# Attention with two MoE-style layers on one core: g_q and g_k issued by ScalarE, the function table loaded by a small first Square, the first pair's roots on VectorE, the second pair's q and k loaded ahead of v

## The chip, the cores and the metric

The program runs on one core of one Trainium2 chip. The metric is device time in microseconds (us) of one execution. The time before is 1150.96 us, the median of three runs (1147.56 to 1157.47).

## What is computed

Attention with normalized q and k, and then two feed-forward layers over its output.

```python
# q, k, v: (4, 12, 448, 64) float32; g_q, g_k: (64,)
def rmsnorm(x, g):
    return x / np.sqrt(np.mean(x * x, axis=-1, keepdims=True) + 1e-06) * g
scores = (q_n @ k_n.T) / sqrt(64)          # q_n = rmsnorm(q, g_q), k_n = rmsnorm(k, g_k)
attn = softmax(scores);  x = attn @ v      # per batch and head
x = x.transpose(0, 2, 1, 3).reshape(1792, 768)
h = x @ moe_w_in;   g = h * sigmoid(1.702 * h);                      x = g @ moe_w_out
h = x @ moe2_w_in;  g = max(h, 0) + moe2_alpha * min(h, 0);          out = g @ moe2_w_out
```

The four weight matrices (768 x 2048 into a layer, 2048 x 768 out of it) come in as 64-bit floats, all other inputs as 32-bit floats.

## The kernel before

**Tiles and stages.** Heads are handled in pairs: a batch of 12 heads has 6 pairs, and one pair's q and k make one tile `qk` of 128 partitions x 2 heads x 7 column groups x 64. The first batch's attention is computed in 32-bit floats, the later batches' in halves of 16 bits. The weights are read as 32-bit words (`weights`, from line 203; a load is issued at line 223), converted by ScalarE and VectorE into 32-bit floats (`from_words`: lines 148, 164, 165), measured by row (line 245), and split into a high and a low 16-bit part (lines 179, 180). The loop over the first batch's first half units is woven with the conversion of the first weight matrix, three steps of it for each attention step; the maximum of v for the later batches is measured in between (lines 312, 314). Then the first feed-forward layer, the other batches' attention beside it, and the second layer follow.

**The first microseconds.** The program makes the identity and the ones, loads the first pair's q and k (`load_qk`, four DMAs, lines 378 to 381), then calls `gains`, which loads g_q and g_k to all partitions (lines 282, 283), multiplies them (284), takes the largest product (287), makes a power of two of it and its reciprocal (105, 106, 112, 113), scales the product (293), and has TensorE transpose it into a column `g_col` (296, 297). v of the first pair comes next (`load_v`, lines 394 to 397), then the second pair's q and k, its v, and the weights. `normalize(0)` squares the first pair's q and k on ScalarE (line 421, two halves), adds them up on VectorE (423), and takes inverse roots on GpSimd by three Newton steps, 14 small operations (424 to 434). `prep_pair(0)` multiplies q and k by the roots (`qn`, line 458), transposes them on TensorE (465, 467), evacuates them on ScalarE with `g_col` as the scale (468), and takes the maximum of v on VectorE (470). The scores (516) follow.

**What sets the order.** All loads at the head go through SyncE's queue, which issues in order; a DMA whose buffer is not free, or that must wait for another, holds all those behind it. On each engine the instructions run in the order in which they were issued, and that order is not the written one: the program is traced in its written order, and a planner (`schedule_with_timeline_sim=True`) places the instructions of each engine by a timeline of its own, the earlier written first among those that are ready there. `issue_after` ties an instruction behind another; the loads that measure v wait so for the roots of pair 4. ScalarE's function table is loaded by an instruction that the build puts ahead of the first activation.

Of the kernel before, what the change touches and what calls it, by code (L numbers as in the profile page):

```python
# [9 lines left out]
F32 = mybir.dt.float32  # L10
# [47 lines left out]
def attention_moe_kernel(  # L58
# [220 lines left out]
    def gains():  # L279
        gq = small.tile([128, D], F32, tag="gq", name="gq", bufs=1)  # L280
        gk = small.tile([128, D], F32, tag="gk", name="gk", bufs=1)
        nc.sync.dma_start(out=gq, in_=g_q.partition_broadcast(128))
        nc.sync.dma_start(out=gk, in_=g_k.partition_broadcast(128))
        nc.vector.tensor_tensor(out=gq, in0=gq, in1=gk, op=ALU.mult)
        gm = small.tile([128, 1], F32, tag="gm", name="gm", bufs=1)
        gi = small.tile([128, 1], F32, tag="gi", name="gi", bufs=1)
        nc.vector.tensor_reduce(out=gm, in_=gq, op=ALU.max, axis=AX, apply_absolute_value=True)
        pow2floor(c_s, gm)
        scaled_reciprocal(gi, c_s, 0.5)
        nc.vector.memset(gs[64:128, 3], 1.0)  # L290
        for c in range(4):
            ps = slice(0, 64 if c == 3 else 128)
            nc.vector.tensor_scalar(out=gs[ps, c], in0=gq[ps], scalar1=gi[ps], scalar2=None, op0=ALU.mult)
        nc.vector.tensor_scalar(out=c_s, in0=c_s, scalar1=2.0 ** -22, scalar2=None, op0=ALU.mult)
        gt = ps_m.tile([128, 128], F32, tag="m", name="gt")
        nc.tensor.transpose(out=gt, in_=gs[:, 0:2].rearrange("p c d -> p (c d)"), identity=identf)
        nc.scalar.activation(out=g_col, in_=gt[:, 0:1], func=AF.Copy, scale=c_s)
# [111 lines left out]
    def normalize(*Ps):  # L409

        Ps = [P for P in Ps if P < B * NP]
        if not Ps:
            return
        n = NT2
        w = 2 * n * len(Ps)
        ss = small.tile([128, 4 * NT2], F32, tag="ss", name="ss")[:, 0:w]
        for t, P in enumerate(Ps):
            flat = raws[P].rearrange("p h c d -> p (h c) d")
            for i in range(2):
                sq = att_p.tile([128, n, D], F32, tag="sq", name="sq", bufs=SQB)  # L420
                nc.scalar.activation(out=sq, in_=flat[:, i * n:(i + 1) * n], func=AF.Square, scale=2.0 ** -13)
                o = (2 * t + i) * n
                nc.vector.tensor_reduce(out=ss[:, o:o + n], in_=sq, op=ALU.add, axis=AX)
        nc.gpsimd.tensor_scalar(out=ss, in0=ss, scalar1=1e-6 * 2.0 ** -20, scalar2=None, op0=ALU.add)
        rs = small.tile([128, 4 * NT2], F32, tag="rs", name="rs")[:, 0:w]
        tn = small.tile([128, 4 * NT2], F32, tag="tn", name="tn")[:, 0:w]
        nc.gpsimd.tensor_scalar(
            out=rs.bitcast(I32), in0=ss.bitcast(I32), scalar1=-0.5, scalar2=RSQRT_SEED, op0=ALU.mult, op1=ALU.add
        )
        for _ in range(3):  # L430
            nc.gpsimd.tensor_tensor(out=tn, in0=rs, in1=rs, op=ALU.mult)
            nc.gpsimd.tensor_tensor(out=tn, in0=tn, in1=ss, op=ALU.mult)
            nc.gpsimd.tensor_scalar(out=tn, in0=tn, scalar1=-0.5, scalar2=1.5, op0=ALU.mult, op1=ALU.add)
            rooted[Ps[0]] = nc.gpsimd.tensor_tensor(out=rs, in0=tn, in1=rs, op=ALU.mult)
        for t, P in enumerate(Ps):
            eng = side(P)
            ks = raws[P][:, :, 0:4]
            flat = raws[P].rearrange("p h c d -> p (h c) d")
            root = rs[:, 2 * n * t:2 * n * (t + 1)]
            if P < NP:  # L440
                roots[P] = root
                continue
            eng.tensor_tensor(out=ks, in0=ks, in1=gs.unsqueeze(1).to_broadcast([128, 2, 4, D]), op=ALU.mult)
            eng.tensor_tensor(out=flat, in0=flat, in1=root.unsqueeze(2).to_broadcast([128, 2 * n, D]), op=ALU.mult)
# [737 lines left out]
    if True:  # L1182
        make_identity(nc, ident)
        nc.vector.memset(ones, 1.0)
        nc.vector.tensor_copy(out=identf, in_=ident)
        load_qk(0)
        gains()
        load_v(0)
        load_qk(1)
        load_v(1)  # L1190
        g0 = big.tile([128, KF, 2, S], F16, tag="g", name="g0")
        stage = g0.rearrange("p m e t -> p (m e t)").bitcast(F32)
        parts = stage[:, 0:R1I * 1024].bitcast(I32).rearrange("p (i n t) -> p i n t", i=R1I, t=2)
        raw1o = g0.rearrange("p m e t -> p m (e t)").bitcast(I32)[:, KF - 4 * R1O:, FIRST:].rearrange("p m (n t) -> p m n t", t=2)

        def num1i(j):
            if j == KD - 1:
                return stage[:, 5120:5120 + FF]
            return held.bitcast(F32)[:, (j - 3) * FF:(j - 2) * FF]

        def num1o(j):
            if j == KF - 2:
                return att_p.tile([128, 2 * NT2 * D], F32, tag="ph", name="num1o", bufs=PHB)[:, 0:DM]
            return raw_p.tile([128, 2 * NT2 * D], F32, tag="qk", name="num1o", bufs=QKB)[:, 0:DM]

        w1i_steps = weights(
            moe_w_in, "w1i", lambda: w1i, later_rows(w1i, 3, num1i), lambda t: parts[:, t % R1I], 4, R1I, 2.0 ** -14, scales,
            G1I
        )
        w1o_steps = weights(  # L1210
            moe_w_out, "w1o", lambda: w1o, later_rows(w1o, 2, num1o), lambda t: raw1o[:, 4 * (t % R1O):4 * (t % R1O) + 4], 2,
            R1O, 2.0 ** -25, scales, G1O
        )
        next(w1i_steps)
        normalize(0)
        for _ in prep_pair(0):
            pass
        for P in range(2, 1 + QKB):
            load_qk(P)
        load_v(2)  # L1220
        normalize(1)
        early = measure(1, B - 1, 4)
        for i, _ in enumerate(first_pairs()):
            if i >= 6:
                for _ in range(1):
                    next(early, None)
            for _ in range(W_RATE):
                next(w1i_steps, None)
        for _ in w1i_steps:
            pass  # L1230
        v_scales(0, v0)
        first_x()
        moe1_scales(0)
        for P in range(NP, NP + 2):
            load_qk(P)
            load_v(P)
        n1o = 0
        steps = attention([4 * P + r for P in range(NP) for r in range(2, 4)])
        for i, _ in enumerate(steps):
            pairs = max(0, (i - LAG + 1) // 2)  # L1240
            rows = KF - 2 if pairs >= 4 else (HOLD + pairs * HELD) // (2 * DM) - 2
            while n1o < min(1 + 2 * rows + 3 * (rows // 2), (i + 1) * W1O_RATE, 57):
                next(w1o_steps)
                n1o += 1
            if i >= M_AT and i - M_AT < KF:
                first_in(slice(0, FIRST), i - M_AT, g0)
            for _ in range(2):
                next(early, None)
        while n1o < 57:
            next(w1o_steps)  # L1250
            n1o += 1
        for m in range(len(range(2 * NP + LAG)) - M_AT, KF):
            first_in(slice(0, FIRST), m, g0)
        with tc.issue_after(loads["w1o"][W1O_HOLD].ins):
            normalize(NP, NP + 1)
            for _ in prep_pair(NP):
                pass
            load_qk(NP + 2)
            load_qk(NP + 3)
            load_v(NP + 2)  # L1260
        att_steps = other_batches()
        done = 4 * NP
        late = late_weights(ctx, att)
        for b in range(B):
            last = min(NU, 4 * NP * (b + 2)) + LAG2
            first = done
            got = None
            for i, _ in enumerate(moe1(b) if b else first_moe1(g0)):
                lead = 0 if b else B1_AT
                want = first + (last - first) * min(1.0, max(0.0, i + 1 - lead) / (PACE[b] * TICKS - lead))  # L1270
                while done < min(want, NU + LAG2):
                    next(att_steps)
                    done += 1
                if b == B - 1:
                    for _ in range(1 if i < 2 * KF else 2):
                        if got is None or i >= 2 * KF:
                            got = next(late, None)
        second_layer(late)
# [30 lines left out]
```

## Time and profile before

| what | value |
|---|---|
| median of three runs | 1150.96 us |
| profiled execution, its own time | 1150.36 us |
| span of its profile | 1148.6 us |
| TensorE matmul busy | 1069.4 us, 93% |
| VectorE busy | 802.1 us, 70% |
| ScalarE busy | 693.2 us, 60% |
| GpSimd busy | 179.4 us, 16% |

The span is the time between the first and the last instruction that the profile shows; the profiled execution's own time is 1.8 us longer. PE is TensorE's matmul, PEld its weight load, DVE is VectorE, ACT is ScalarE, POOL is GpSimd, SP is SyncE and SPq its queue of DMA issues. A busy share over the whole span mixes stages of different limits, so the stretches are read one by one.

### The profile page before, as it was taken

How to read it: one execution, taken by the hardware profiler on the slowest of the kernel's cores; microseconds unless marked ns; L12 is line 12 of the kernel's file. 1: busy time of each engine (PE TensorE's matmuls, PEld its weight loads, DVE VectorE, ACT ScalarE, POOL GpSimd, SP SyncE). 2: the span in 40 equal slices, each digit the busy share in tenths (PEclk: the TensorE clock that was granted, in tenths of full speed). 3: DMA queues.
4: the chain of work that ended last, by engine and by line, in shares of the span. 5: the costliest groups of instructions: out<-in, count | busy, mean ns of one | idle time of the engine just before them, and what ended most of it. 6: DMA issues, size and time to landing. Idle time of an engine off the chain costs nothing.

```text
span 1148.6 us, 18408 instructions
## 1 busy us (share of the span) xinstructions
PE 1069.4 (93%) x6753; PEld 585.0 (51%) x6753; DVE 802.1 (70%) x1397; ACT 693.2 (60%) x1452; POOL 179.4 (16%) x364
## 2 busy tenths in 40 slices
PE   4776889898989999999999999999999999999998
PEld 2343457744444445555455455444444477666664
DVE  5979798887879885577534865599976224959341
ACT  4778686888879876688633562356456425756120
POOL 2701003676433342100000000000000000000000
PEclk9978899899999999999999999999999999999999
DMA  7974743478888756455446501765351423363111
GB/s 227 258 178 132 182 129 109 97 158 184 183 191 167 160 130 151 109 121 118 78 124 229 203 1 64 249 215 194 136 171 59 138 70 113 106 184 101 33 31 28
DMA packets 235562, 158.19 MB, mean 138 GB/s; under 512 B 167888, under 2 KB 214736, under 8 KB 235472
## 3 DMA queue, kind: packets, MB, share of 16 engines
q1 hardware_dynamic: 229200, 141.34, 44.6%
q0 software_dynamic: 6272, 15.67, 5.3%
q8 instruction: 53, 0.87, 0.3%
q14 instruction: 37, 0.30, 0.1%
HBM read 92.35 MB, written 25.69 MB: 103 GB/s over the span
## 4 chain that ended last, share of the span: by engine, by line
PE 56%; DVE 16%; DMA 11%; issue 7%; ACT 6%; POOL 4%; SPq 1%; DVEq 0%; POOLq 0%; ACTq 0%
PE op L1090 17%; PE yp L821 15%; PE h L927 9%; PE hp L798 7%; PE xp L648 3%; PE sp L525 2%; DMA t<-hl 2%; PE hp L758 2%; DMA g<-in_moe_w_in_dram 2%; DVE nm L530 1%; DMA g<-in_moe_w_out_dram 1%; DVE g L141 1%; ACT pr L550 1%; DMA qk<-in_q_dram 1%; DMA yr<-y_dram 1%
## 5 line engine op out<-in xcount | busy, mean ns | idle before, releaser
L821 PE MATMUL yp<-g,w1o 128*128 128x448 f16 x1152 | 226.9, 354 | 1.5 <-DVE g L767 0.9
L927 PE MATMUL h<-x,w2i 128*128 128x512 f16 (+1 forms) x1152 | 219.3, 352 | 4.3 <-DVE pos L933 2.8
L798 PE MATMUL hp<-x,w1i 128*128 128x448 f16 x864 | 170.3, 353 | 1.6 <-DVE t L807 1.6
L927 PEld LDWEIGHTS <-w2i 128*128 128x128 f16 x1152 | 112.6, 98 | 109.6 <-issue 5.1
L821 PEld LDWEIGHTS <-w1o 128*128 128x128 f16 x1152 | 109.5, 98 | 110.8 <-issue 12.0
L798 PEld LDWEIGHTS <-w1i 128*128 128x128 f16 x864 | 81.9, 98 | 83.5 <-issue 9.6
L620 DVE SCALAR_TENSOR_TENSOR ph<-pr,sm,ph 128x448 f16<-128x448 f32 x126 | 85.2, 707 | 25.4 <-ACT ph L593 25.4
L530 DVE TENSOR_REDUCE nm<-sp 128x2 f32<-128x896 f32 x96 | 92.5, 964 | 10.3 <-PE sp L525 7.6
L932 ACT ACTIVATE pos<-h,sign 128x512 f32<-128x512 f32 (+1 forms) x64 | 40.1, 628 | 89.7 <-PE h L927 83.3
L550 ACT ACTIVATE pr<-sp,nm,c_s 128x448 f32<-128x448 f32 x126 | 89.9, 717 | 2.4 <-DVE ph L620 1.1
L1090 PEld LDWEIGHTS <-even 128*128 128x128 f16 x672 | 65.7, 98 | 43.5
L933 DVE SCALAR_TENSOR_TENSOR pos<-h,slope,pos 128x512 f32<-128x512 f32 (+1 forms) x64 | 43.4, 680 | 59.9 <-ACT pos L932 59.7
L593 ACT ACTIVATE ph<-pr,sm 128x448 f16<-128x448 f32 x126 | 77.6, 659 | 10.7 <-DVE sm L590 10.6
L758 PE MATMUL hp<-x,w1i 128*128 128x256 f16 (+1 forms) x576 | 66.1, 276 | 9.2 <-DVE g L767 5.2
L1090 PEld LDWEIGHTS <-odd 128*128 128x128 f16 x504 | 49.3, 98 | 32.6
L758 PEld LDWEIGHTS <-w1i 128*128 128x128 f16 x576 | 55.2, 104 | 20.2 <-issue 14.8
L1090 PE MATMUL op<-w2lo,even 128*128 128x384 f16 x384 | 63.5, 326 | 0.0
L648 PE MATMUL xp<-pt,vs 128*64 128x256 f16 (+1 forms) x792 | 49.8, 267 | 7.5 <-DMA pt<-ph 6.2
L525 PE MATMUL sp<-t 64*128 64x448 f16 (+1 forms) x432 | 54.0, 357 | 0.6 <-DMA t<-hl 0.5
L648 PEld LDWEIGHTS <-vs 128*64 128x64 f16 x792 | 37.9, 112 | 27.6 <-issue 17.2
L532 ACT ACTIVATE nm<-nm,c_s 128x2 f32<-128x2 f32 x72 | 20.9, 290 | 48.5 <-DVE nm L530 48.1
L1090 PE MATMUL op<-w2hi,even 128*128 128x384 f16 x288 | 47.5, 326 | 0.0
(243 smaller groups left out, 1659.7 us busy)
## 6 DMA issues: line engine op xcount, KB each, us to landing
g<-in_moe_w_in_dram SPq DMA_DIRECT2D x24, 512.0 KB, 6.1
g<-in_moe_w_out_dram SPq DMA_DIRECT2D x32, 384.0 KB, 4.0
w2raw<-in_moe_w_in_dram SPq DMA_DIRECT2D x24, 512.0 KB, 5.7
w2raw<-in_moe_w_out_dram SPq DMA_DIRECT2D x16, 768.0 KB, 6.4
g_dram<-pos SPq DMA_DIRECT2D x48, 256.0 KB, 2.0
gp<-g_dram SPq DMA_DIRECT2D x8, 1024.0 KB, 6.8
odd<-g_dram SPq DMA_DIRECT2D x6, 1024.0 KB, 5.5
y_dram<-y SPq DMA_DIRECT2D x24, 224.0 KB, 2.5
```

Source lines behind the costliest of these rows:

```text
L525: nc.tensor.matmul(out=sp[:, j, 0:S] if n == 2 else sp[ds, 0, 0:S], lhsT=qt[ds] if n == 2 else qt[ds, 64:128], rhs=kt[ds, 0:S], start=(i = ...
L530: nc.vector.tensor_reduce(out=nm[:, 0:n], in_=sp[:, 0:n, 0:S], op=ALU.max, axis=AX, negate=True)
L550: last = nc.scalar.activation(out=pr[i], in_=sp[:, i, 0:S], func=AF.Exp, bias=nm[:, i:i + 1], scale=c_s if u >= 4 * NP else 1.0, accum_out ...
L593: nc.scalar.activation(out=ph[:, i, 0:S], in_=pr[i], func=AF.Copy, scale=sm[:, i:i + 1])
L620: nc.vector.scalar_tensor_tensor(out=ph[:, i, S:2 * S], in0=pr[i], scalar=sm[:, i:i + 1], in1=ph[:, i, 0:S], op0=ALU.mult, op1=ALU.subtract)
L648: nc.tensor.matmul(out=xp[64 * j:64 * j + 64, t:t + n], lhsT=vs[ks, j, c], rhs=pt[ks, 7 * j + kc, 0:n] if b else pt[ks, kc, o:o + n], star ...
L758: nc.tensor.matmul(out=ps, lhsT=w1i[:, kk, e, m * 128:(m + 1) * 128], rhs=xs[0, kk][:, f, cols], start=(i == 0), stop=(i == 3 * KD - 1))
L798: nc.tensor.matmul(out=ps, lhsT=w1i[:, kk, e, m * 128:(m + 1) * 128], rhs=x[:, f], start=(n == 0), stop=(n == 3 * KD - 1))
L821: nc.tensor.matmul(out=ps, lhsT=w1o[:, m, e, j * 128:(j + 1) * 128], rhs=g[:, m, f], start=(n == 0), stop=(n == 3 * KF - 1))
L927: nc.tensor.matmul(out=ps, lhsT=w2i[:, kk, e, m * 128:(m + 1) * 128], rhs=x2[kk][:, f], start=(c == 0), stop=(c == 3 * KD - 1))
L933: nc.vector.scalar_tensor_tensor(out=pos, in0=ps, scalar=slope[:, m:m + 1], in1=pos, op0=ALU.mult, op1=ALU.max)
L1090: nc.tensor.matmul(out=ps, lhsT=ops[:, o, m, f], rhs=rhs[:, e], start=(c == 0), stop=(c == 3 * KH - 1))
```

## The change

Four edits. `gains` issues the loads of g_q and g_k from ScalarE's queue, no longer from SyncE's, and is called after `normalize(0)` instead of after `load_qk(0)`. The first pair's roots are computed by VectorE; the other pairs' stay on GpSimd. One Square of a single column of the ones, into a new tile `first`, is written ahead of all other work of ScalarE. The second pair's q and k are loaded in front of the first pair's v.

```diff
@@ gains
-        nc.sync.dma_start(out=gq, in_=g_q.partition_broadcast(128))
-        nc.sync.dma_start(out=gk, in_=g_k.partition_broadcast(128))
+        nc.scalar.dma_start(out=gq, in_=g_q.partition_broadcast(128))
+        nc.scalar.dma_start(out=gk, in_=g_k.partition_broadcast(128))
@@ normalize
-        nc.gpsimd.tensor_scalar(out=ss, in0=ss, scalar1=1e-6 * 2.0 ** -20, scalar2=None, op0=ALU.add)
+        eng = nc.vector if Ps[0] < 1 else nc.gpsimd
+        eng.tensor_scalar(out=ss, in0=ss, scalar1=1e-6 * 2.0 ** -20, scalar2=None, op0=ALU.add)
...
-        nc.gpsimd.tensor_scalar(
+        eng.tensor_scalar(
             out=rs.bitcast(I32), in0=ss.bitcast(I32), scalar1=-0.5, scalar2=RSQRT_SEED, op0=ALU.mult, op1=ALU.add
         )
         for _ in range(3):
-            nc.gpsimd.tensor_tensor(out=tn, in0=rs, in1=rs, op=ALU.mult)
-            nc.gpsimd.tensor_tensor(out=tn, in0=tn, in1=ss, op=ALU.mult)
-            nc.gpsimd.tensor_scalar(out=tn, in0=tn, scalar1=-0.5, scalar2=1.5, op0=ALU.mult, op1=ALU.add)
-            rooted[Ps[0]] = nc.gpsimd.tensor_tensor(out=rs, in0=tn, in1=rs, op=ALU.mult)
+            eng.tensor_tensor(out=tn, in0=rs, in1=rs, op=ALU.mult)
+            eng.tensor_tensor(out=tn, in0=tn, in1=ss, op=ALU.mult)
+            eng.tensor_scalar(out=tn, in0=tn, scalar1=-0.5, scalar2=1.5, op0=ALU.mult, op1=ALU.add)
+            rooted[Ps[0]] = eng.tensor_tensor(out=rs, in0=tn, in1=rs, op=ALU.mult)
@@ the start of the program
         nc.vector.memset(ones, 1.0)
+        first = small.tile([128, 1], F32, tag="first", name="first", bufs=1)
+        nc.scalar.activation(out=first, in_=ones[:, 0:1], func=AF.Square)
         nc.vector.tensor_copy(out=identf, in_=ident)
         load_qk(0)
-        gains()
+        load_qk(1)
         load_v(0)
-        load_qk(1)
         load_v(1)
...
         normalize(0)
+        gains()
         for _ in prep_pair(0):
             pass
```

## Rows read from the trace of the kernel before

**Rows 1.** The page's part 2: TensorE's busy tenths, 40 equal slices of the span.

```profile
PE   4776889898989999999999999999999999999998
```

**Rows 2.** Stretches: length; busy of PE, PEld, DVE, ACT, POOL; clock, DMA, GB/s.

```profile
0.00:10.00 10.00, 0.00 (x0) 0.00 (x0) 2.42 (x10) 2.33 (x3) 1.16 (x8) 1.00 0.45 123
...
10.00:20.00 10.00, 5.10 (x15) 2.72 (x17) 6.55 (x16) 4.60 (x9) 6.28 (x26) 1.00 0.89 306
...
20.00:40.00 20.00, 11.87 (x37) 5.23 (x34) 19.50 (x32) 14.74 (x30) 8.88 (x24) 1.00 0.95 282
...
400.00:1148.60 748.60, 736.90 (x4399) 395.29 (x4397) 467.47 (x751) 382.14 (x724) 28.19 (x59) 1.00 0.41 122
```

**Rows 3.** Timeline, 0 to 45 us, SyncE's queue: start, duration, line, transfer, count.

```profile
3.21 0.59 SPq L282 DMA_DIRECT2D gq<-in_g_q_dram  x1
...
3.84 0.43 SPq L283 DMA_DIRECT2D gk<-in_g_k_dram  x1
...
4.32 0.43 SPq L394 DMA_DIRECT2D w1o<-in_v_dram  x1
...
6.10 0.59 SPq L378 DMA_DIRECT2D qk<-in_k_dram  x1
...
8.55 0.59 SPq L394 DMA_DIRECT2D w1o<-in_v_dram  x1
...
10.59 2.57 SPq L223 DMA_DIRECT2D g<-in_moe_w_in_dram  x5
```

**Rows 4.** Timeline, 0 to 45 us, compute engines; in brackets idle, its releaser.

```profile
4.79 1.28 ACT L421 ACT_TABLE_LOAD   x1 [4.79 <-DMA qk<-in_q_dram]
...
6.09 1.04 ACT L421 ACTIVATE sq<-qk 128x448 f32<-128x448 f32 x2
...
6.70 0.62 DVE L423 TENSOR_REDUCE ss<-sq 128x7 f32<-128x448 f32 x1 [5.13 <-ACT sq L421]
...
8.60 0.23 DVE L284 TENSOR_TENSOR gq<-gq,gk 128x64 f32<-128x64 f32 x1 [1.28 <-DMA gk<-in_g_k_dram]
...
8.74 0.61 DVE L423 TENSOR_REDUCE ss<-sq 128x7 f32<-128x448 f32 x1
...
9.45 0.26 POOL L424 TENSOR_SCALAR ss<-ss 128x14 f32<-128x14 f32 x1 [8.15 <-DVE ss L423]
...
9.52 0.15 DVE L105 TENSOR_SCALAR c_s<-gm 128x1 f32<-128x1 f32 x1
...
9.70 0.15 DVE L106 TENSOR_SCALAR c_s<-c_s 128x1 int32<-128x1 int32 x1
...
10.00 0.69 DVE L470 TENSOR_REDUCE v<-w1o 128x1 f32<-128x512 f32 x1
...
10.79 0.76 DVE L293 TENSOR_SCALAR gs<-gq,gi 128x64 f32<-128x64 f32 x4
...
13.34 0.22 POOL L434 TENSOR_TENSOR rs<-tn,rs 128x14 f32<-128x14 f32 x1
...
13.59 1.09 DVE L458 TENSOR_TENSOR qn<-qk,rs 128x896 f32<-128x896 f32 x1 [0.39 <-POOL rs L434]
...
20.67 0.67 ACT L148 ACTIVATE w1i<-g 128x512 f32<-128x512 f32 x1 [0.92 <-DMA g<-in_moe_w_in_dram]
```

**Rows 5.** DMA view, 4.2 to 6.6 us: GB/s in slices; a transfer to landing.

```profile
GB/s 21 4 17 13 26 21 21 26 26 21 21 17 30 17 26 26 17 26 21 17 26 17 4 17 17 17 21 13 47 30 34 30 26 17 13 26 4 0 4 13
...
w1o<-in_v_dram SPq DMA_DIRECT2D x1, 192.0 KB, 5.0
```

**Rows 6.** DMA view, 10 to 24 us: large part of v, us to landing.

```profile
w1o<-in_v_dram SPq DMA_DIRECT2D x1, 192.0 KB, 2.7
```

**Rows 7.** Waits of SyncE's queue, 0 to 120 us: total, times, longest.

```profile
SPq L129 <- DMA line<-am: 7.2, 1, 7.2
```

**Rows 8.** Timeline, 62 to 100 us, VectorE's two idle times.

```profile
78.84 0.29 DVE L134 TENSOR_REDUCE a<-row 128x1 f32<-128x128 f32 x1 [3.04 <-DMA row<-line]
...
82.36 0.43 DVE L164 TENSOR_SCALAR g<-g 128x512 int32<-128x512 int32 x1 [2.78 <-ACT g L148]
```

## The prediction

> **What bounds the kernel now.** I read the page's slices first. From about the fifteenth slice on, TensorE shows 9 in nearly every slice [rows 1]; the first ten hold the holes. The table by stretches puts numbers to it [rows 2]: from 400 us to the end TensorE is busy 736.90 of 748.60 us at a granted clock of 1.00. No row of that stretch is touched by the change, so a saving at the head reaches the end only as a shift of everything behind it, and nearly undiminished if it survives to there. In the first 20 us no engine is near full (TensorE 5.10 us, VectorE 2.42 and 6.55), while DMA goes from 0.45 to 0.89. From 20 to 40 us VectorE is busy 19.50 of 20 and DMA 0.95: the weights' conversion and the attention both hang on VectorE there, and the loads feed them. So the head is a latency chain, then comes a stretch held by VectorE and loads together, then TensorE.
>
> The timeline of the head gives the chain [rows 4]. ScalarE's load of the function table begins at 4.79 us, when the first pair's q and k are there, and the first squares start at 6.09. VectorE reduces the first half at 6.70, then stands until 8.60 before it multiplies g_q by g_k, and only at 8.74 reduces the second half. GpSimd makes the roots from 9.45 to 13.56 and VectorE scales the pair (qn) from 13.59. This same view shows that the written order is not the issued one: the gains are written ahead of the sums, yet the first sum was issued ahead of the product. A planner places what its own timeline calls ready, and I keep that in mind for every "behind" in the change.
>
> The third view is SyncE's queue [rows 3]: one issue after another of about 0.6 us, g_q and g_k at 3.21 and 3.84, the first v at 4.32, the second q and k from 6.10, the first weights at 10.59. So g_k took from 3.84 to 8.60 to be of use. The DMA view of 4.2 to 6.6 us shows about 20 GB/s [rows 5], and the first v's large part took 5.0 us to land, where the second's took 2.7 [rows 6].
>
> **The change part by part, and the sum.**
>
> *Table first.* The load takes 1.28 us [rows 4]. It moves in front of the landing: the new Square needs only the ones, and ScalarE's queue otherwise holds the two DMA issues, 0.59 and 0.43 us on SyncE [rows 3]. Behind two issues that start at about 0.75 us, load and Square (at most the 0.52 us of one big square) end by about 3.6 us, 1.2 us ahead of the landing at 4.79, which hides them. If that cover were gone, at most 0.5 us would come back. Saved for the first squares: 6.09 - 4.79 - 0.02 = 1.28 us. The squares start 0.02 us after the load ends. The Trainium skill, "ScalarE: Activation LUTs", section "What ACT_TABLE_LOAD costs", states 1283 ns for the load, as here, and a drain of 1380 ns besides; by it the saving would be 2.66 us, but this trace shows no such drain ahead of the squares.
>
> *Gains to ScalarE's queue.* SyncE loses two issues: 4.32 - 3.21 = 1.11 us for all that follows in its order [rows 3]. The bounds are nothing, if the two queues share what makes the descriptors and each delays the other, and 1.11 us plus the 2.3 us (5.0 - 2.7) that the first v lay behind g_q and g_k [rows 5, 6]. I take 1.11: SyncE issues steadily at 0.6 us apiece, and the hole at 4.2 to 6.6 was partly just its low bytes per issue.
>
> *Second q, k ahead of v.* The second pair's four issues start at 3.21 instead of 6.10, 2.9 us earlier. The first v goes from 4.32 past four issues (8.55 - 6.10 = 2.45 us) and gains 1.11, so 5.66, 1.3 us later [rows 3]. Its only early reader is a maximum on VectorE at 10.00 [rows 4]; its last small part is issued near 7.0 and at 2.7 us a load is there at 9.7, so it waits at most 0.7 us if the planner still places it that early, and with 5.0 us up to 2.0. The second v and the weights gain the 1.11 us. I set this at zero for the first pair.
>
> *Product out of the way, roots on VectorE.* Without its wait, the second sum follows the first at once: the squares start at 4.81, the first sum at 5.42 (0.61 later, as before), two sums of 0.62 and 0.61 end at 6.65 instead of 9.35. That is 2.70 us, the table's 1.28 in it. The roots are 14 small dependent operations, 4.11 us on GpSimd. VectorE has no such row; its nearest are the dependent scalings of 128x1 in the same chain, 9.52 to 9.70, 0.18 us apart, and I allow 0.20 for 14 columns: 2.8 us. The lower bound is 14 times 0.15 = 2.1 us (no gap between them), the upper 4.11 (no better than GpSimd). Gain 1.3 (0 to 2.0). Then the product's chain: between 8.60 and 11.55 VectorE ran its 11 operations, 1.9 us of busy time, beside GpSimd's roots. That cover is gone, since both are now on VectorE: it costs 1.9 us if all stands ahead of qn, 0 if it fills gaps between the dependent root steps. I take 1.9. First qn: 13.59 - 2.70 - 1.3 + 1.9 = 11.5 us, 2.1 us earlier; bounds 0.8 and 4.7. What waits behind VectorE's roots is only the product, qn and the second sums, whose roots stay on GpSimd and are no longer queued behind the first pair's.
>
> *What of it arrives.* At 20.67 us ScalarE waits 0.92 us for a weight's landing [rows 4], and DMA is at 0.89, then 0.95. There loads end last, and these gain 1.11 us, not 2.1. I take the smaller: the saturated VectorE stretch begins 1.1 us earlier, and the shift goes through. The profiled execution took 1150.36 us (span 1148.6), 0.6 below the median of 1150.96: 1150.36 - 1.1 = **1149.3 us**.
>
> **Rivals.**
>
> *Nothing arrives.* The Trainium skill, "DMA: Bandwidth & Descriptors", section "Issuing engines are not separate DMA queues", says that a second issuing engine saves only the time of initiating, and that all transfers interleave on the same 16 engines. Here that would be: g_q and g_k, which held the first v by 2.3 us on one queue, hold the first q and k instead. They would land at 7.1, the second sum end at 7.1 + 1.84 = 8.94, roots at 11.7, qn with the product at 13.6, as before; the loads' 1.1 us then finds VectorE not ready. For it: the 20 GB/s; against: another queue need not wait for one whose transfers are slow. 1150.4 us.
>
> *The change does not do what it says.* The planner, seeing g_k ready early from ScalarE, places the product's 11 operations ahead of the sums. VectorE then waits for the true landing, 1.3 + 4.7 = 6.0, ends the product at 7.9, sums at 9.2, roots at 12.0: qn 1.6 us earlier instead of 2.1. Loads still decide, 1149.3, or 1150.4 where the first v's maximum also gets in front.
>
> *Slower: a stall in SyncE's queue is dealt again.* At 67 to 75 us SyncE stands 7.2 us for a small store's landing before it may read it back [rows 7], with weight loads behind it; VectorE then idles 3.04 and 2.78 us [rows 8], 5.8 in all. Its place is the planner's choice, and the planner gets other ready times. If such a wait falls once more ahead of weight loads, the price is 5.8: 1150.4 - 1.1 + 5.8 = 1155 us. It decides as soon as VectorE's idle time up to the end of the first weights grows by more than 1.1 us. For it: the first sum's place shows how the order follows ready times; against: that store is written far behind the head.
>
> *Faster: the same stall falls where nothing waits.* 1150.4 - 1.1 - 5.8 = 1143.5 us.
>
> **How the numbers follow.** The forecast has 0.48, nothing arrives 0.17, the product placed ahead 0.12, the stall again 0.13, the stall gone 0.10. The forecast's own range, from the bounds above, is 1150.4 less 0 to 4.7: 1145.7 to 1150.4. To hold 8 in 10 I reach to both stall cases and add the runs' own spread to the slow side (1157.47): **1142 to 1158**. One per cent, 11.5 us, is about what a measurement of this kernel can tell from no change, and none of my priced cases reaches it. What is left for more than that is a reorder larger than any I priced: faster 0.05, within 0.90, slower 0.05.
>
> **What would show it.** Table load by 3.6 us and squares at 4.8 us: the first step. Squares later than 6 us: the contention rival. Sums done by 6.7, roots' 14 operations in about 2.8 us on VectorE, qn at 11.5. The first weight load issued at 9.5 instead of 10.59, and VectorE's full stretch starting 1.1 us earlier. If the first 20 us come out so and the end differs by more than 5 us, the order further back was dealt anew, and VectorE's idle time between 60 and 200 us will show where. I would be wrong in kind if TensorE's busy time from 400 us on changed, since nothing here touches it.

## The result: half a per cent slower, and where it lies

| | before | after |
|---|---|---|
| median of 11 runs each | 1149.72 us (1146.41 to 1157.47) | 1157.39 us (1152.18 to 1162.48) |
| ratio, 95% interval | | 1.0052 [1.0030, 1.0074] |
| the same again, later runs (34 and 11) | 1152.73 us | 1159.97 us, 1.0056 [1.0032, 1.0080] |
| span of the profiled execution | 1148.6 us | 1156.2 us |

The forecast was 1149.3 us, a little faster. The kernel became slower, by 6 us by the ratio and by 7 to 8 by the medians: inside the range, on the other side.

**The head.** The timeline of after's first 45 us, DMA issues (start, duration, queue, line, transfer), against [rows 3]:

```profile
0.72 0.43 ACTq L282 DMA_DIRECT2D gq<-in_g_q_dram  x1
...
1.25 0.40 ACTq L283 DMA_DIRECT2D gk<-in_g_k_dram  x1
...
3.20 0.60 SPq L378 DMA_DIRECT2D qk<-in_k_dram  x1
...
5.70 0.60 SPq L381 DMA_DIRECT2D qk<-in_q_dram  x1
...
7.03 0.37 SPq L394 DMA_DIRECT2D w1o<-in_v_dram  x1
...
10.69 2.71 SPq L223 DMA_DIRECT2D g<-in_moe_w_in_dram  x5
```

The same timeline, compute engines, against [rows 4]:

```profile
1.18 1.28 ACT L1187 ACT_TABLE_LOAD   x1 [1.18 <-PEq L1296]
...
2.48 0.20 ACT L1187 ACTIVATE first<-ones 128x1 f32<-128x1 bf16 x1
...
6.44 0.23 DVE L284 TENSOR_TENSOR gq<-gq,gk 128x64 f32<-128x64 f32 x1 [4.88 <-DMA gk<-in_g_k_dram]
...
7.55 1.04 ACT L421 ACTIVATE sq<-qk 128x448 f32<-128x448 f32 x2 [4.87 <-DMA qk<-in_q_dram]
...
8.38 1.13 DVE L423 TENSOR_REDUCE ss<-sq 128x7 f32<-128x448 f32 x2
...
9.54 0.17 DVE L425 TENSOR_SCALAR ss<-ss 128x14 f32<-128x14 f32 x1
...
14.07 0.17 DVE L435 TENSOR_TENSOR rs<-tn,rs 128x14 f32<-128x14 f32 x1
...
14.28 1.09 DVE L459 TENSOR_TENSOR qn<-qk,rs 128x896 f32<-128x896 f32 x1
...
18.13 1.08 DVE L459 TENSOR_TENSOR qn<-qk,rs 128x896 f32<-128x896 f32 x1
```

The table is loaded by 2.46, but the squares begin at 7.55, not 6.09: with g_q and g_k in flight from the other queue, the first q and k are there 2.8 us later than the 4.79 of before. The DMA view of 0 to 10 us shows it (GB/s in slices of 0.25 us, before, then after):

```profile
GB/s 0 0 0 0 0 0 0 43 132 261 332 338 363 105 100 43 112 14 23 23 22 24 11 29 26 11 18 30 143 183 116 154 243 312 307 328 345 294 216 219
```

```profile
GB/s 0 0 0 0 0 0 0 9 7 54 80 117 119 104 143 115 106 116 19 117 215 159 144 302 356 356 327 277 240 179 143 111 107 83 332 261 88 69 119 11
```

From 2.25 to 3.25 us after moves 54 to 119 GB/s where before moved 261 to 363, and the second pair's first load is issued only at 3.20. The product stands ahead of the sums. The 14 root steps take from 9.54 to 14.24, since sums and maxima were placed between them. So the first qn is 0.7 us later than in [rows 4], the second comes at 18.13. The first weight load is issued at 10.69, against 10.59: SyncE's queue stands 0.7 us ahead of 5.70 and 0.7 us ahead of 7.03, for landings of k and q, which it did not do before, and that uses up the two issues saved.

**The stretches**, columns as in [rows 2]; then TensorE's tenths, as [rows 1]:

```profile
0.00:10.00 10.00, 0.48 (x1) 0.18 (x1) 3.79 (x19) 3.78 (x7) 0.68 (x6) 1.00 0.46 125
10.00:20.00 10.00, 3.94 (x12) 2.21 (x14) 9.08 (x24) 3.55 (x7) 4.54 (x14) 1.00 0.89 302
20.00:40.00 20.00, 12.68 (x45) 6.32 (x42) 18.82 (x30) 15.39 (x33) 10.58 (x28) 0.62 0.94 280
400.00:1156.20 756.20, 743.34 (x4452) 398.69 (x4449) 470.25 (x758) 387.91 (x739) 27.87 (x59) 1.00 0.43 122
```

```profile
PE   3876897889899999999999999999999999999998
```

The granted clock of 20 to 40 us is 0.62, where it was 1.00; VectorE is the fuller engine there, and nothing of that is left at 250 us (below). From 400 us on TensorE idles 12.9 us, where it idled 11.7; 53 more of its matmuls are left for that stretch. SyncE's stall of [rows 7] is 8.8 us now; of VectorE's two waits [rows 8] one of 4.41 us is left in place of 5.8 in all. None of the places that the prediction named holds the loss. I paired VectorE's instructions of the two traces, the n-th of each kind with the n-th: after's are 0.8 us ahead around 250 us, 3.7 behind around 350, 11.5 around 450. This is the stretch in which the other batches' attention runs beside the first layer's second product, and there one wait of TensorE is worth reading: for `pt`, which a transposing DMA fills from `ph` (lines 628 and 633, SyncE's queue). `ph` holds a unit's softmax in two 16-bit parts, and `pt` is its transpose, as the product with v needs it; `hl` and `t` are the same pair for q and k, and `vs` holds v in its parts.

### The profile page after: what moved, and what is told of

It reads as the page before. It is cut to its first block, busy times and chain, and to the rows that moved or that the text cites. A ratio compares the mean times of both kernels' runs of the same rounds, so it can differ in the third digit from the quotient of the medians.

```text
span 1156.2 us, 18398 instructions
## 1 busy us (share of the span) xinstructions
PE 1070.1 (93%) x6753; PEld 583.9 (51%) x6753; DVE 803.4 (69%) x1411; ACT 691.0 (60%) x1453; POOL 176.1 (15%) x350
## 4 chain that ended last, share of the span: by engine, by line
PE 53%; DVE 16%; DMA 12%; ACT 8%; issue 6%; POOL 3%; SPq 1%; ACTq 0%; DVEq 0%; POOLq 0%
PE op L1091 17%; PE yp L822 13%; PE h L928 9%; PE hp L799 6%; DMA qk<-in_q_dram 3%; PE xp L649 3%; DMA g<-in_moe_w_in_dram 3%; ACT pr L551 2%; PE sp L526 2%; DMA g<-in_moe_w_out_dram 2%; DMA t<-hl 2%; PE hp L759 2%; DVE ph L621 1%; DMA yr<-y_dram 1%; DVE w2num L165 1%
## 5 line engine op out<-in xcount | busy, mean ns | idle before, releaser
L759 PE MATMUL hp<-x,w1i 128*128 128x256 f16 (+1 forms) x576 | 62.9, 268 | 10.1 <-DVE g L768 4.4
```

The costliest lines, as they stand in the source:

```text
L759: nc.tensor.matmul(out=ps, lhsT=w1i[:, kk, e, m * 128:(m + 1) * 128], rhs=xs[0, kk][:, f, cols], start=(i == 0), stop=(i == 3 * KD - 1))
```

## Experiments

Where an expectation speaks of an order written out, the issue order of each engine was read from a built program and each instruction tied behind its forerunner, by a table:

```diff
         attention_moe_kernel(tc, *args)
+        _in_order(tc, _TABLE)
...
+        if e in last:
+            tc.add_manual_dep(i, last[e], mybir.DependencyInfo(
+                mybir.DependencyClass.NoSync, mybir.DependencyReason.DATA), reason="order")
```

Kernels that only add the Square or an unused buffer need none of this: there every other instruction kept its place by itself.

**1. Edits against order, crossed.** My first theory was the planner's order far behind the head, the rival the edits themselves. The changed source with one table, then the source of before with another:

> All four edits and the issue order that the changed kernel has up to about 25 us, but behind that, on every engine, the issue order of the kernel before, written out instruction by instruction. Theory (the loss is in the order that the planner dealt anew far behind the head): the loss is gone, within 0.2% of the kernel before (1147.5 to 1152 where that is 1149.7). Rival (the edits themselves, g_q and g_k holding the first q and k, cost the time on the chip): about +0.5%, as the changed kernel, near 1157.

Measured 1.0081 [1.0049, 1.0114]. Not the theory: with the old order the loss is no smaller.

> None of the edits, and the kernel before's own issue order up to about 25 us; behind that, on every engine, the issue order of the changed kernel, written out. Theory (the later order costs it): +0.5% although not one edit is in it, near 1157. Rival (the edits cost it): as the kernel before, within 0.2%.

Measured 1.0032 [1.0011, 1.0054]: slower without a single edit, as the theory has it, by two thirds of what was expected. Order and edits (or something that comes with them) each cost.

**2. Single edits.**

```diff
+        first = small.tile([128, 1], F32, tag="first", name="first", bufs=1)
+        nc.scalar.activation(out=first, in_=ones[:, 0:1], func=AF.Square)
```

> The kernel before with the one small Square ahead of all else and nothing more; the issue order of every other instruction stays as it was. Theory: the first squares start at 4.8 us instead of 6.09; g_q times g_k still waits for g_k (8.60), so qn gains at most 0.1 us and the end 0 to 0.5 us: 1149.2 to 1149.7, within 0.1% of before. Rival (what the head gains or loses is multiplied behind it): a change of over 2 us.

Measured 1.0089 [1.0060, 1.0119], a miss for the theory: 0.20 us of work in an idle stretch, no other instruction in another place, and 10 us are lost. Its trace is 0.7 us ahead of before at 250 us and 14.7 us behind at 450.

```diff
-        gains()
         load_v(0)
...
         normalize(0)
+        gains()
```

> The kernel before with the call of the gains moved behind the first normalize and nothing else (g_q and g_k still on SyncE's queue, now behind v's and the second q's loads); the planner deals the whole order anew. Theory: the head moves by at most 2 us, yet the end may move by several us either way, since the later order is another one: outside 1148 to 1152 more likely than inside, and where the time goes lies behind 100 us. Rival (only the head's hardware effect counts): within 2 us of before.

Measured 1.0113 [1.0083, 1.0144]. It separates little: my figure for the head was wrong, since g_q's load, now behind v's, the second q's and the weights' waits, is issued at 12.31 us, the product comes at 21.86 and g_col at 32.76. VectorE is some 8 us behind before already around 200 us, so most of this loss lies ahead of the stretch named above, and it is not explained here.

**3. Something inert in place of the Square.** In the built programs `first` takes 32 bytes of each partition ahead of nearly all working buffers, and moves them: `ph` from 218112 to 218144, `hl` from 178176 to 178208, `pt` from 188928 to 188960 (a buffer's address is called its place below). So a buffer without a Square:

```diff
+        spare = small.tile([128, 1], F32, tag="spare", name="spare", bufs=1)
+        nc.gpsimd.memset(spare, 0.0)
```

> The kernel before with one more buffer of one 32-bit column, cleared by GpSimd, at the place where the changed kernel has its small Square; no Square, no other edit, the issue order of all other instructions the same. In the built program the new buffer takes 32 bytes of each partition and moves all buffers behind it, those into which the transposes and the loads of q, k and v land among them, from multiples of 64 bytes to 32 past one. New theory (the moved buffers cost the time, since every run with the small buffer shows DMA busier in 240 to 430 us for the same bytes: 64.5 to 68.3% against 58.9 to 59.7%): +0.6 to +1.0%, as the Square alone. Rival (the Square or the table load did it): within 0.2% of before.

Measured 1.0073 [1.0045, 1.0101]: a buffer without a Square costs what the Square did.

```diff
-        first = small.tile([128, 1], F32, tag="first", name="first", bufs=1)
+        first = small.tile([128, 16], F32, tag="first", name="first", bufs=1)[:, 0:1]
```

> The kernel before with the small Square alone, as in the run that was 0.89% slower, but its buffer is 16 columns wide (64 bytes of each partition, one column written), so the buffers behind it move by 64 bytes and stay multiples of 64. New theory (the place of the buffers): the loss is gone, -0.1 to +0.1% against before. Rival (the Square, the earlier table load): +0.9% as measured with the narrow buffer.

Measured 1.0067 [1.0042, 1.0092]. Multiples of 64 are not enough. The same edit in the changed kernel, and in the first kernel of 1:

> The changed kernel, all its edits and its own issue order, with the small Square's buffer 16 columns wide. New theory: the part of the loss that the buffers' place makes goes away, and what is left is what the planner's other order and the head make, 0 to +0.35% (the changed order behind the old head measured +0.32%). Rival (the place matters only with the old order): +0.5% as the changed kernel.

> All four edits, the issue order of the kernel before behind the head, and the buffer of 16 columns: the run that was 0.81% slower, with its buffers back on multiples of 64 bytes. New theory: -0.2 to +0.1%, what the four edits are worth by themselves. Rival (the edits' head, g_q and g_k ahead of the first q and k, costs it): still +0.5 to +0.8%.

Measured 1.0077 [1.0047, 1.0107] and 1.0065 [1.0036, 1.0094], both misses for the same reason.

**4. No buffer moved.** The Square writes into g_col, which exists:

```diff
-        first = small.tile([128, 1], F32, tag="first", name="first", bufs=1)
-        nc.scalar.activation(out=first, in_=ones[:, 0:1], func=AF.Square)
+        nc.scalar.activation(out=g_col, in_=ones[:, 0:1], func=AF.Square)
```

> The kernel before with the small Square alone, but it writes into g_col, a buffer that is there already and is written again later; no buffer moves, and the issue order of all other instructions is that of before. Theory now (any shift of the buffers behind the new one, by 32 or by 64 bytes, slows the transposes between 240 and 450 us; in the kernel before, ph, pt and hl begin at multiples of 512 bytes): -0.15 to +0.1%, transposes' median landing 3.8 us or less in 240 to 430 us. Rival (the Square itself): +0.9%.

Measured 1.0011 [0.9987, 1.0035], against 1.0089 with the buffer. The same edit in the first kernel of 1, then in the changed kernel:

> All four edits, the issue order of before behind the head, no buffer moved: what the edits are worth by themselves. The head of the changed kernel brings the first pair's qn 0.7 us later and the second's 2.3 us earlier. Theory: -0.2 to +0.1%. Rival (g_q and g_k ahead of the first q and k cost the end): +0.5% or more.

Measured 0.9996 [0.9972, 1.0021], against 1.0081: all four edits, and nothing lost.

> The changed kernel, all its edits and its own issue order; only the small Square's result goes into g_col, so every buffer lies where it lay before the change. Theory: most of the +0.5% goes away; 0 to +0.35% is left for the planner's other order (the changed order behind the old head measured +0.32%). Rival (the order or the edits alone): +0.5% as the changed kernel.

Measured 1.0042 [1.0018, 1.0065], more than I expected: with the new order most of the loss stays.

**5. Which bytes, and whose.**

```diff
+        spare = small.tile([128, 32], F32, tag="spare", name="spare", bufs=1)
+        nc.gpsimd.memset(spare[:, 0:1], 0.0)
```

> The kernel before with an unused buffer of 32 columns (128 bytes of each partition, one column cleared by GpSimd): all buffers behind it move by 128 bytes; nothing else changes. If what counts is a grain of 128 bytes or less other than 32 and 64: within 0.2% of before, transposes landing in 3.8 us. If it is 256 or 512 bytes: +0.6 to +0.9% and 4.3 us, as with 32 and 64 bytes.

Measured 1.0042 [1.0018, 1.0067], below the 0.6 to 0.9% expected though the interval reaches into it; the signs in the trace are those of 32 and 64.

With 64 columns in place of 32:

> As the moves by 32, 64 and 128 bytes, now by 256: the sources of the transposes (ph, hl) then begin at multiples of 256 but no longer of 512 bytes. If 256 is the grain: within 0.2% of before, shortest issue of the transposes of hl 1.47 us, copies of vs always about 0.6 us. If 512: +0.4 to +0.9%, 1.52 us and about 1.1 us in half of them.

Measured 0.9989 [0.9964, 1.0014], and no sign of it in the trace: the grain is 256 bytes. The buffer and its clearing are in this kernel too, so it is the place that costs. Then an unused buffer of 32 bytes just ahead of the first buffer in the place of `ph`, or (the same line) of `pt`:

```diff
+                nc.gpsimd.memset(att_p.tile([128, 8], F32, tag="gap", name="gap", bufs=1)[:, 0:1], 0.0)
                 return att_p.tile([128, 2 * NT2 * D], F32, tag="ph", name="num1o", bufs=PHB)[:, 0:DM]
```

> The kernel before with an unused buffer of 32 bytes (one column cleared by GpSimd) just ahead of ph alone: of all buffers only ph, from which the transposes read, and num1o, which shares its place, move by 32 bytes; the order is that of before. If the place that the transposes read from counts: +0.5 to +0.9%, the transposes' landing in 240 to 430 us at 4.3 us or more, and issues of the copy of vs at about 1.1 us. If it doesn't: within 0.2%, 3.8 us, 0.6 us.

> As the run before, but the unused buffer lies ahead of pt: pt, vs, t1 and ph move by 32 bytes, while hl, the buffers of q, k and v and all smaller ones stay. If the transposes' landing places (pt, t1) count: +0.5 to +0.9%, with landings of 4.3 us or more, also where moving ph alone did nothing. If neither counts: within 0.2%, and the cause is among the buffers that stayed.

Measured 1.0037 [1.0011, 1.0063] and 1.0046 [1.0021, 1.0072]. Both are less than expected. Moving `ph` alone already costs; that moving `pt` besides adds to it is not shown, nor whether `ph` is all of the 0.73%.

**6. What is left.** The source of before, with a table of both orders:

> None of the edits, no buffer moved; the order of before up to about 240 us (TensorE's 1242nd matmul) on every engine, the changed kernel's order behind. If the other order costs its 0.3 to 0.4% behind 240 us, where the traces of both kernels with that order lose (between 330 and 440 us): +0.25 to +0.5%. If the part ahead of 240 us counts: within 0.15% of before.

Measured 1.0048 [1.0022, 1.0075]: the order behind 240 us alone makes all of the order's share. The order ahead of it was not run by itself. The changed kernel, unedited, beside the moved `ph` and `pt`:

> The changed kernel as it is, against the same runs of before as its neighbours here: +0.4 to +0.8%, that is, not the sum of the place alone (+0.7 to +0.9%) and the other order alone (+0.42%), which would be +1.1 to +1.3%.

Measured 1.0056 [1.0032, 1.0080]: the two causes do not add up (0.73 and 0.42 would be 1.15%). Last, the changed source with a table of its own, and:

```diff
-        nc.scalar.dma_start(out=gq, in_=g_q.partition_broadcast(128))
-        nc.scalar.dma_start(out=gk, in_=g_k.partition_broadcast(128))
+        nc.sync.dma_start(out=gq, in_=g_q.partition_broadcast(128))
+        nc.sync.dma_start(out=gk, in_=g_k.partition_broadcast(128))
...
-        nc.scalar.activation(out=first, in_=ones[:, 0:1], func=AF.Square)
+        nc.scalar.activation(out=g_col, in_=ones[:, 0:1], func=AF.Square)
```

> A version meant to be better than both: the small Square into g_col (no buffer moves), the first pair's roots on VectorE straight behind its sums, then qn, then the gains' product; g_q and g_k back on SyncE's queue behind the first q and k; the second q and k ahead of v; behind the head the order of before. First squares at 4.8, qn at 9.6 to 10 us instead of 13.59, the second qn 3 us earlier. If the head's gain arrives: -0.2 to -0.4%. If it is absorbed between 60 and 380 us, as the edits' 2 to 4 us were: within 0.15% of before.

Measured 1.0009 [0.9981, 1.0037]. The timeline of its head:

```profile
4.92 1.04 ACT L421 ACTIVATE sq<-qk 128x448 f32<-128x448 f32 x2 [2.70 <-DMA qk<-in_q_dram]
...
6.71 0.17 DVE L425 TENSOR_SCALAR ss<-ss 128x14 f32<-128x14 f32 x1
...
9.42 0.17 DVE L435 TENSOR_TENSOR rs<-tn,rs 128x14 f32<-128x14 f32 x1
...
9.63 1.09 DVE L459 TENSOR_TENSOR qn<-qk,rs 128x896 f32<-128x896 f32 x1
...
13.14 1.04 ACT L421 ACTIVATE sq<-qk 128x448 f32<-128x448 f32 x2
...
15.39 0.66 ACT L148 ACTIVATE w1i<-g 128x512 f32<-128x512 f32 x1 [0.68 <-DMA g<-in_moe_w_in_dram]
```

The first qn is 4.0 us earlier than before; behind 20 us VectorE is 0.0 us ahead. ScalarE still waits for a weight's landing at 15.39, and the second squares stand behind g_col until 13.14. No version here beats before by more than the noise.

### How the place costs, read from the traces

SyncE's queue around 320 us, before (start, duration, line, transfer), then the kernel with the inert buffer (its lines count one more), then the one moved by 256 bytes:

```profile
321.38 1.50 SPq L480 DMA_TRANSPOSE t<-hl  x1
325.13 0.62 SPq L485 DMA_DIRECT2D vs<-vs  x1
...
336.85 1.48 SPq L480 DMA_TRANSPOSE t<-hl  x1
```

```profile
329.14 1.55 SPq L481 DMA_TRANSPOSE t<-hl  x1
332.91 1.15 SPq L486 DMA_DIRECT2D vs<-vs  x1
...
345.71 1.54 SPq L481 DMA_TRANSPOSE t<-hl  x1
349.47 1.07 SPq L486 DMA_DIRECT2D vs<-vs  x1
```

```profile
325.77 0.60 SPq L486 DMA_DIRECT2D vs<-vs  x1
...
337.12 1.48 SPq L481 DMA_TRANSPOSE t<-hl  x1
```

The shortest issues of the transposes of `hl` are 1.47 to 1.48 us in these kernels when the source begins at a multiple of 256 bytes, and 1.52 to 1.54 when it does not; the copy of `vs` behind the transposes takes over 0.9 us in 9 of 18 cases with the inert buffer, in 1 of 18 before. With `ph` alone moved, the transposes of `hl` keep their 1.48, and 9 copies of the unmoved `vs` are long: what counts for an issue is its source's place, and the copy only stands behind the transposes. For `ph` itself the sign is as small and is not in all issues: the median of those of line 627 of before goes from 1.49 to 1.56 us, while those of line 632, which take half the partitions, stay at 1.26 and 1.27. The DMA view of 240 to 430 us, before and then with the inert buffer (the queue's packets, MB, share of the engines' time; transposes, count and median us to landing):

```profile
q1 hardware_dynamic: 86244, 23.16, 59.7%
...
pt<-ph SPq DMA_TRANSPOSE x51, 3.8
...
t<-hl SPq DMA_TRANSPOSE x10, 3.7
```

```profile
q1 hardware_dynamic: 84252, 22.46, 65.7%
...
pt<-ph SPq DMA_TRANSPOSE x50, 4.3
...
t<-hl SPq DMA_TRANSPOSE x10, 4.3
```

Fewer packets and fewer bytes, and more time for them. Over the whole program the packets are the same in number, and the two pages have:

```profile
q1 hardware_dynamic: 229200, 141.34, 44.6%
```

```profile
q1 hardware_dynamic: 229200, 141.34, 46.7%
```

This share parts all traces: 44.1 to 45.0% in the nine with all sources at multiples of 256, whatever the order, and 46.3 to 47.8% in the eleven with a source 32, 64 or 128 bytes past one. The Trainium skill, "DMA: Bandwidth & Descriptors", section "How a descriptor splits into AXI transactions", says that each transaction begins at a multiple of 256 bytes, and that a piece which does not begin there pays for bytes that are fetched and not used. These runs agree: moves by 32, 64 and 128 bytes cost, one by 256 does not. The Trainium skill, the same page, section "Constraints", asks a transpose for 32-byte alignment; all these kernels keep it, and here it is not enough for full speed.

TensorE's waits of 240 to 460 us (total, times, longest): before; moved by 256; inert buffer; only the new order from 240 us on; after.

```profile
PE xp L648 <- DMA pt<-ph: 6.2, 3, 3.2
```

```profile
PE xp L649 <- DMA pt<-ph: 7.1, 3, 3.1
```

```profile
PE xp L649 <- DMA pt<-ph: 14.9, 5, 5.8
```

```profile
PE xp L648 <- DMA pt<-ph: 12.0, 8, 3.4
PE sp L525 <- ACT pr L550: 2.2, 3, 0.9
PE yp L821 <- ACT g L140: 1.8, 1, 1.8
```

```profile
PE xp L649 <- DMA pt<-ph: 8.4, 7, 1.9
PE xp L649 <- DVE ph L621: 2.5, 1, 2.5
PE yp L822 <- ACT g L140: 1.4, 1, 1.4
```

The inert buffer adds 8.7 us of waiting for `pt`, about its whole loss of 0.73%, 8.4 us. With every buffer where it was before, the new order makes TensorE wait for `pt` more often (8 times, not 3). This wait varies from one execution to the next: after, with 8.4 us here, shows 13.7 in its other profiled execution (`i3`), and the last kernel of 6, which loses nothing by its median, shows 11.5 in an execution 4.1 us above that median. In the twelve other kernels with the order of before, what an execution waits for `pt` beyond 6.2 us is within 3 us of what it takes beyond 1150.36, but for one (the first kernel of 1: 3.7 and 8.5). With the new order it is looser: 2.2 and 7.6 us in after, 7.5 and 7.7 in its other execution. Both causes lengthen this one wait, and a transpose that is needed later can also land later: I read this as the reason that they do not add up, but no run tests it. TensorE's busy time in these 220 us falls with it: before, inert buffer, new order from 240 us on.

```profile
240.00:460.00 220.00, 211.25 (x1512) 104.49 (x1507) 173.61 (x297) 183.89 (x446) 98.00 (x182) 0.98 0.76 167
```

```profile
240.00:460.00 220.00, 203.31 (x1437) 99.86 (x1435) 167.18 (x285) 176.55 (x430) 93.79 (x172) 0.96 0.81 160
```

```profile
240.00:460.00 220.00, 203.42 (x1438) 99.99 (x1437) 166.78 (x285) 175.93 (x432) 95.23 (x175) 0.97 0.76 158
```

How far VectorE's instructions run behind those of before (us, medians around the time of before; minus is ahead):

| kernel | order of before? | sources on 256? | 20 us | 250 | 290 | 350 | 450 | 650 |
|---|---|---|---|---|---|---|---|---|
| moved by 256 | yes | yes | 0.0 | -0.5 | +0.2 | +0.7 | +0.4 | +0.6 |
| inert buffer | yes | no | -0.1 | 0.0 | +6.0 | +9.2 | +12.2 | +10.2 |
| four edits | yes | yes | -2.3 | -3.7 | -1.5 | -0.9 | +1.3 | +0.6 |
| four edits, 64 bytes | yes | no | -2.4 | -3.0 | +6.3 | +10.1 | +13.0 | +10.7 |
| new order from 240 us | no | yes | +0.1 | -2.5 | -4.1 | +3.8 | +7.9 | +7.6 |
| after | no | no | -2.3 | -0.8 | -1.4 | +3.7 | +11.5 | +8.9 |
| last kernel of 6 | yes | yes | 0.0 | +0.2 | +2.5 | +7.5 | +9.2 | +8.1 |

One profiled execution carries much chance. The kernel moved by 256 bytes, without an edit, is 1.9 us ahead around 200 us and level at the end, and the last row is the slow execution just named, of a kernel that measured 1.0009. So what each cause is worth stands on the ratios of experiments 3 to 6, and these rows only show where an execution loses.

## Why the prediction was wrong, step by step

*Table first.* The load was out of the way by 2.46 us, within the 3.6 foretold. The squares did not begin at 4.81, since q and k were late. Where they were less late, they began at 4.92 (the last kernel of 6) and 5.33 (the Square alone). The step failed in what it left out: I priced the small Square by its time on ScalarE and not by its buffer. Those 32 bytes alone are worth +0.73% with the order of before.

*Gains to ScalarE's queue.* I took 1.11 us and had "nothing" as the other end; nothing it was (10.69 against 10.59), and with it went the 1.1 us of the sum, which was this term and no other. And the rival's mechanism was there: g_q and g_k held the first q and k. I had 7.1 us for their landing; the squares show 7.55. The Trainium skill, "DMA: Bandwidth & Descriptors", section "Issuing engines are not separate DMA queues", which I had quoted for that rival, says that all transfers interleave on the same engines. This trace agrees: 54 to 119 GB/s from 2.25 to 3.25 us, where before had 261 to 363.

*Product out of the way, roots on VectorE.* The planner placed the product ahead of the sums, which I gave 0.12. The 14 steps took 4.7 us with other work between them; placed together they took 2.88 (6.71 to 9.59), against my 2.8. The size was right, the order was not mine to assume.

*What of it arrives.* That the loads decide held: with qn 4.0 us earlier and the weights issued at 10.48, nothing arrives behind 20 us, and the four edits with order and place kept are worth 0.9996 [0.9972, 1.0021]. The 1.1 us that I forecast lies inside that interval, so its sign is not settled.

*The sentence that failed* is in the first part: no row from 400 us on is touched by the change, so a saving "reaches the end only as a shift of everything behind it". The change touched every row from the head on, in two ways that the diff does not show: it dealt the issue order anew (+0.42% [0.18, 0.65] with no buffer moved; by the order behind 240 us alone +0.48% [0.22, 0.75]), and it moved the buffers. In the changed kernel the second is not told apart from nothing once the first is there (1.0052 and 1.0056, and 1.0077 with the wider buffer, against 1.0042; all intervals overlap). The sign that I had given for being wrong in kind came: TensorE's busy time from 400 us on went from 736.90 to 743.34 us, since more of its work was left for then. The two stall rivals had the kind of the first cause, a wait dealt anew, but not its place: I looked at SyncE between 67 and 75 us, and it was TensorE's wait for `pt` between 240 and 460. What in that order makes `pt` late more often stays open. That 1157 lies inside the range is luck: its slow end was put there for SyncE's stall falling once more, with VectorE idle behind it, and of those waits of VectorE 4.41 us are left in place of 5.8.

## What to carry to other kernels

Before pricing an edit at the head of a planned kernel, ask what it does to issue order and to buffer addresses everywhere; a tile of four bytes can cost more than the edit can bring. Test an edit with order and addresses held as they were, and judge the new order and the new places by themselves. Let the source of a transposing DMA begin at a multiple of 256 bytes; here a scratch result written into an existing buffer kept that for nothing.

## What the runs showed that I had not expected

Sources 32, 64 or 128 bytes past a multiple of 256 make the same 229200 packets on SyncE's queue take 46.3 to 47.8% of the DMA engines' span in place of 44.4 to 45.0%. And two loads of 256 bytes, spread to all partitions by another queue, put off four larger ones by 2.8 us.
